# Extra matmuls on TensorE whose results nobody reads: behind every argument matmul, and in four places before, between and after other work

## The chip, the core and the metric

The kernel runs on one core of one Trainium2 chip. The metric is the device time of one execution in microseconds; lower is better. Engines are named as in the profile: PE is TensorE's matmuls, PEld its weight loads, DVE VectorE, ACT ScalarE, POOL GpSimd, SP SyncE. A line such as L748 is a line of the kernel before.

## The reference

Two branches over the same input `x` (2048 positions, 640 channels) are mixed by a gate per position. Branch A is attention with 32 heads of 20 channels, where each position sees 8 earlier ones at a distance of 2. Branch B is a state-space convolution: a kernel K of 2048 taps per channel is made from 192 complex modes, and is convolved with the input by FFT.

```python
g = sigmoid((x * gate_w).sum(-1, keepdims=True))
# A: q, k, v = x @ wqkv; 8 taps, dilation 2; softmax over the taps; @ wo
idx = pos[:, None] - off[None, :]            # off = arange(8) * 2
logits = einsum("bhsd,bhswd->bhsw", q, k[idx]) * scale
a = einsum("bhsw,bhswd->bhsd", softmax(logits), v[idx]) @ wo
# B: K[d, l] = Re sum_n C[d,n] exp(dt[d] A[d,n] l) dt[d] B[d,n]
P = exp((dt * A)[:, :, None] * arange(L))
K = einsum("dn,dnl,dn->dl", C, P, dt * B).real
b = irfft(rfft(pad(x)) * rfft(pad(K)))[:L] + x * Dskip
return g * a + (1 - g) * b
```

## The kernel before

**Two plans.** The program has two parts. The first holds the projections, the attention, the making of K and the first step of the transform. The second, `fft_conv`, holds the rest of the transform, the product of the spectra, the inverse and the mix. Each part is a list of tasks (`Plan.add`), each task with an engine (P is TensorE, A ScalarE, D VectorE, S and G the queues of SyncE and GpSimd), a function that issues its instructions, and tasks that it depends on. The order in which all tasks are issued is written out by hand as a list of task numbers, `SEQ1` for the first part and `SEQ2` for the second. Every engine runs its instructions strictly in that order. The numbers after a task's name (duration, `eq`, `due`) served to find an order, and change nothing in what is issued.

**The making of K.** The 80 channel groups are taken in 10 chunks (`NCH`). For each chunk, TensorE makes the arguments of sine and exponential functions by small matmuls (`args`, L747): the stationary operand is a slice of `L`, 64 rows and 128 columns, the moving operand a slice of the constant `R`. A task of kind 0 (sine) issues two matmuls of `SW` = 304 columns, one for each half of the array's rows, into the two banks of a tile `ar` of 2 x 512 fp32 values. A task of kind 1 (exponential) issues four of `EW` = 216 columns, two into each bank. There are 12 tasks of kind 0 and 6 of kind 1 in each chunk, 180 in all. ScalarE then evaluates the function from `ar` (`act`, L760 for the sine, L762 for the exponential) and writes into a ring of buffers. VectorE multiplies sine and exponential tiles (L783 to L785), and TensorE sums the products over the modes in many small matmuls on 32 columns of the array (L801).

There are two tiles `ar` at a time. They are also used for the transposes of the input (L200), for the gate's logits, and for the first step of the transform (`bp`, L1232). So TensorE can be at most two tiles ahead of the engine that reads them.

**The attention** runs in between. The projections are at L291 (tile `tb`, 512 columns, five accumulated matmuls for each tile). The logits (L357), the softmax's shift (L379) and its sum (L387) go to the tile `lg`, the sum over the taps (L426) and the output projection (L444) again to `tb`. `ident` is the identity matrix, 128 x 128.

**The shapes of the array.** A matmul of 128 rows and 128 columns is shown as 128*128. L748 uses 64 rows at a time (64*128, with `tile_position`), L801 and L357 use 32 columns, L426 uses 64 columns.

**The end of the first part.** K's two halves go through device memory (`Kx`, then `kc`), and the first step of the transform reads them from there (L1232). Then `fft_conv` starts with L1009.

## Time and profile before

| | |
|---|---|
| median of 3 runs | 362.78 us (361.1 to 363.49) |
| the profiled execution's own time | 360.97 us |
| its span, first to last instruction | 359.0 us |
| mean granted clock of TensorE | 0.961 |
| busy: PE, DVE, ACT, POOL | 293.7, 311.5, 303.0, 78.3 us |
| the 480 argument matmuls (L748) on PE | 55.3 us busy, idle before them 14.7 us |
| the sine activations (L760, 96 of 120) on ACT | 59.0 us busy, 681 ns each |
| the exponential activations (L762, 60) on ACT | 50.3 us busy, 917 ns each |

The busy time of an engine is the union of its instructions' times. A matmul's end is modelled, and matmuls overlap, so the distance between the starts of two groups tells more than the length of one. In the timelines, a row is a run of like instructions: its start, its length, the engine, the line, the operation, what it writes and reads with the shape of the array, the count, and in brackets how long the engine was idle before it and what ended that. In a row of groups, the numbers after the bar are the busy time in microseconds and the mean length of one instruction in nanoseconds, then the idle time before them. A row of waits tells who waited for whom: total time, how often, the longest.

### The profile page before, as it was taken

The page shows a single profiled execution, that of the slowest core. Times are in us where ns is not written, and L with a number is a line of the kernel's source. Part 1 is how long each engine was busy: PE and PEld are TensorE (multiplying, and loading weights), DVE is VectorE, ACT ScalarE, POOL GpSimd, SP SyncE. Part 2 cuts the span into 40 slices and gives each one's busy share as a digit, 9 for nine tenths or more (in the row PEclk, how much of TensorE's full clock was granted, in tenths as well). Part 3 has the DMA queues.
Part 4 walks back from the last instruction along what each step waited for, and adds up shares of the span by engine and source line. Part 5 has one row for each costly group of instructions (what it writes and reads, how often), then busy time and mean ns, then how long its engine had stood idle before and what let it go on. Part 6 is the DMA issues. An engine that isn't in the chain of part 4 may idle for free. (4 is left out here: it accounts for less than half of the span.)

```text
span 359.0 us, 12203 instructions
## 1 busy us (share of the span) xinstructions
PE 293.7 (82%) x5271; PEld 173.4 (48%) x5286; DVE 311.5 (87%) x413; ACT 303.0 (84%) x417; POOL 78.3 (22%) x125
## 2 busy tenths in 40 slices
PE   0199999699999999888887869999997799978760
PEld 0065564234544545445443424566664556647650
DVE  2899999669999899999998987999993479999982
ACT  1699997578989999999997979999895599888881
POOL 8930090211020100100012122416010023310032
PEclk9999999989999999999998978999998899999995
DMA  7951289421501611461256867489653149943047
GB/s 259 370 175 57 82 213 268 120 66 19 150 11 27 122 40 19 140 129 30 71 109 192 190 152 137 95 177 256 172 153 101 38 126 225 228 95 75 4 98 199
DMA packets 44042, 46.60 MB, mean 130 GB/s; under 512 B 24517, under 2 KB 38133, under 8 KB 43733
## 3 DMA queue, kind: packets, MB, share of 16 engines
q1 hardware_dynamic: 36116, 24.43, 26.2%
q0 software_dynamic: 5840, 20.55, 22.5%
q10 hardware_dynamic: 2032, 0.85, 0.9%
q8 instruction: 41, 0.67, 0.8%
q14 instruction: 13, 0.10, 0.1%
HBM read 31.31 MB, written 14.51 MB: 128 GB/s over the span
## 5 line engine op out<-in xcount | busy, mean ns | idle before, releaser
L291 PE MATMUL tb<-bufA 128*128 128x512 bf16 x285 | 71.7, 387 | 2.8 <-issue 1.1
L748 PE MATMUL ar<-Rarg,L 64*128 64x304 bf16 (+1 forms) x480 | 55.3, 282 | 14.7 <-ACT big L760 5.9
L760 ACT ACTIVATE big<-ar 128x608 bf16<-128x608 int16 x96 | 59.0, 681 | 8.2 <-PE ar L748 5.7
L762 ACT ACTIVATE big<-ar 128x864 bf16<-128x864 f32 x60 | 50.3, 917 | 3.6 <-PE ar L748 3.3
L291 PEld LDWEIGHTS <-bufA 128*128 128x128 bf16 x300 | 33.2, 120 | 31.7 <-issue 9.3
L420 DVE TENSOR_TENSOR pv<-vc,asb 128x4096 bf16<-128x4096 bf16 (+1 forms) x24 | 46.3, 1928 | 1.4 <-PE tb L426 1.4
L748 PEld LDWEIGHTS <-L 64*128 64x128 bf16 x480 | 21.4, 94 | 48.8 <-issue 41.9
L1009 PEld LDWEIGHTS <-PHI 128*128 128x128 bf16 x288 | 26.8, 99 | 18.0 <-issue 8.4
L801 PE MATMUL kps<-qq,pt 128*32 128x22 bf16 (+1 forms) x2560 | 26.3, 175 | 4.2 <-issue 4.2
L444 PE MATMUL tb<-wo_sb,oT 128*128 128x320 bf16 x160 | 28.1, 311 | 0.0
L801 PEld LDWEIGHTS <-pt 128*32 128x32 bf16 (+1 forms) x2560 | 22.5, 91 | 11.6 <-issue 8.7
L351 DVE TENSOR_TENSOR prod<-qk 128x2048 bf16<-128x2048 bf16 x20 | 24.1, 1220 | 2.9 <-PE lg L357 2.8
L351 DVE TENSOR_TENSOR prod<-prj 128x2048 bf16<-128x2048 bf16 x20 | 24.0, 1219 | 0.6 <-PE lg L357 0.5
L345 POOL DMA_DIRECT2D vc<-vS x16 | 11.5, 725 | 57.1 <-DVE pv L420 54.0
L426 PE MATMUL tb<-pv,ind 128*64 128x512 bf16 (+1 forms) x192 | 22.4, 361 | 0.2
L785 DVE TENSOR_TENSOR qq<-big 128x1408 bf16<-128x1408 bf16 x24 | 21.2, 885 | 0.0
L470 ACT ACTIVATE bufA<-bp 128x1024 bf16<-128x1024 f32 x16 | 16.0, 1032 | 5.6 <-PE bp L1232 5.5
L1009 PE MATMUL fp<-big,PHI 128*128 128x320 bf16 x112 | 17.9, 304 | 3.0 <-ACT sp_u L470 3.0
L200 PE MATMUL ar<-ident,xn 128*128 128x128 bf16 x80 | 8.1, 263 | 15.0 <-DMA xn<-in_A_x_dram 14.3
L470 ACT ACTIVATE sp_u<-fp 128x1280 bf16<-128x1280 f32 x14 | 17.3, 1237 | 3.4 <-PE fp L1009 3.4
L470 ACT ACTIVATE prj<-tb 128x512 bf16<-128x512 f32 x28 | 17.1, 612 | 3.1 <-PE tb L291 3.0
L470 ACT ACTIVATE big<-bp 128x1024 bf16<-128x1024 f32 x19 | 18.6, 1023 | 1.0 <-PE bp L1232 0.8
(173 smaller groups left out, 587.2 us busy)
## 6 DMA issues: line engine op xcount, KB each, us to landing
vc<-vS POOLq DMA_DIRECT2D x16, 327.5 KB, 6.9
PHI<-c_phi POOLq DMA_DIRECT2D x8, 384.0 KB, 4.9
Sprm<-pc SPq DMA_DIRECT2D x12, 240.0 KB, 2.0
L<-Sprm SPq DMA_DIRECT2D x80, 36.0 KB, 2.6
xn<-in_A_x_dram SPq DMA_DIRECT2D x4, 640.0 KB
gaS<-ga SPq DMA_DIRECT2D x8, 320.0 KB, 3.0
Usb<-in_A_x_dram POOLq DMA_DIRECT2D x8, 320.0 KB, 5.0
gaF<-gaS SPq DMA_DIRECT2D x8, 320.0 KB, 7.3
```

The costliest lines, as they stand in the source:

```text
L291: nc.tensor.matmul(ppf, self.wq[:, kt, which * D + e:(which + 1) * D:5], self.xT[:, c0 // 1024, kt, c0 % 1024:c0 % 1024 + SC], start=(kt = ...
L351: nc.vector.tensor_tensor(b[e][:], self.part(ch, 0)[:, e, o:o + C].unsqueeze(1).to_broadcast([128, W, C]), win(self.part(ch, 1)[:, e, :], ...
L420: nc.vector.tensor_tensor(b["pv", e][:, 0:2 * n], taps, aw, ALU.mult)
L426: nc.tensor.matmul(b["op", e][64 * a:64 * a + 64, 0:n, :], self.twin, b["pv", e][:, a:2 * n:2, w, :], start=(w == 0), stop=(w == HV - 1), ...
L444: nc.tensor.matmul(apf[:, :320], b["oT"][:, e, i * 128:(i + 1) * 128], wo_sb[:, e, hf * 320:(hf + 1) * 320], start=(e == 0), stop=(e == 4))
L470: nc.scalar.activation(o, i, ACT.Identity)
L748: nc.tensor.matmul(ar[:, g2, a0:a0 + ncol], L[rows, sb, gp, l0:l0 + 128], R[rows, c0:c0 + ncol], start=True, stop=True, tile_position=(64 ...
L760: nc.scalar.activation(dst[:, 2 * gp:2 * gp + 2, sub, :], ar[:].bitcast(I16)[:, :, 0:2 * SW:2], ACT.Sin, scale=SCL)
L762: nc.scalar.activation(dst[:, 2 * gp:2 * gp + 2].rearrange("p g s n -> p g (s n)"), ar[:, :, 0:2 * EW], ACT.Exp)
L785: nc.vector.tensor_tensor(qq[:], trg[:, :, KI:].rearrange("p a (v m) -> p a v m", v=2), exq[:, :, KI:].unsqueeze(2).to_broadcast([128, 32, ...
L801: nc.tensor.matmul(kps[32 * g:32 * g + 32, h, NM * ql:NM * ql + NM], pt[rows, k, v, :], qq[rows, k, v, :], start=(g not in started), stop= ...
L1009: nc.tensor.matmul(o.rearrange("p (c x) -> p c x", x=32), phis[fb][:, fl, kind, :], B[:, :, 2 * f1 + ri].rearrange("p c q g -> p c (q g)") ...
```

## The change

Behind the argument matmuls of each task comes, in the columns of the tile `ar` that stay free, a matmul with the identity as stationary operand and the constant `R` as moving operand: for kind 0 one of 512 - 304 = 208 columns in the second bank, for kind 1 one of 512 - 432 = 80 columns in each of the two banks. These use the whole array (no `tile_position`). Nobody reads what they write.

Besides, four new tasks (`fl0` to `fl3`, numbers 1090 to 1093 in `SEQ1`) each take a tile `ar` and write four matmuls of 512 columns into it. In the order, the first stands just ahead of the first argument task, the second and third behind the last group of L426, and the fourth at the end of the first part, behind the last L1232 and ahead of L1009. The rest of the order is the same; in the diff, the list is only broken into lines anew.

```diff
@@ SEQ1 @@
-... 517 244 563 562 245 518 520 268 ...
+... 517 244 563 562 245 1090 518 520 268 ...
-... 504 500A 1059A 1053A 505 503A 506D 1074 1070 ...
+... 504 500A 1059A 1053A 505 1091 1092 503A 506D 1074 1070 ...
-... 515 1078 1086 1079D 1087A
+... 515 1078 1086 1079D 1087A 1093
@@ args @@
                                         nc.tensor.matmul(ar[:, g2, a0:a0 + ncol], L[rows, sb, gp, l0:l0 + 128], R[rows, c0:c0 + ncol],
                                                          start=True, stop=True, tile_position=(64 * g2, 0))
+                                for g2 in (1,) if kind == 0 else (0, 1):
+                                    o = (SW, 2 * EW)[kind]
+                                    nc.tensor.matmul(ar[:, g2, o:512], self.ident[:], R[:, 0:512 - o], start=True, stop=True)
                                 b["ar", u, kind, gp, sub] = ar
@@ gated_mix_kernel @@
+        kg.ident = at.ident
         kg.plan(pl, pa, pk, lambda c: pr["g"][c], late[:30] + xdone[-1:], params, opened, fin)
...
+        def warm(_):
+            w = pa.tile([128, 2, 512], F32, name="ar")
+            for k in range(4):
+                nc.tensor.matmul(w[:, k % 2], at.ident[:], kg.R[:, 0:512], start=True, stop=True)
+        for n in range(4):
+            t = pl.add(f"fl{n}", "P", 0.85, warm, acq=["ar"], due=0.0, eq=2176)
+            t.rel = [("ar", t)]
         pl.emit(tc)
```

More of the change, by code (lines that the diff above doesn't have):

```diff
@@ L65 @@
 60 62D 122 146 85A 123A 57 147A 91A 125 129 230 126A 61 63 112 48 130A 113A 50 231 59 64A 152 154 153A 65A 155A 67 139 222 232 66 233 49 58 69 54 140A 68 70 55 71 72 234
-127 137 73 235 128A 236 143 237 138A 223 144A 516 238 133 265 239 131 134D 240 148 267 224 132A 241 242 150 225 149A 151A 226 243 266 269 517 244 563 562 245 518 520 268
-141 270 519 521 271 522 524 272 523 273 994 124 221 145 228 264 156 525 274 526 528 167 275 301 168D 142A 527 529 276 530 532 531 533 178 534 536 180 535 537 179A 303 538
@@ L68 @@
-540 539 541 175 181D 246 176D 186 542 544 277 278 543 545 187A 279 182 546 548 302 304 157 554 305 307 547 183A 549 158A 159 184 160A 306 308 550 552 551 553 185D 309 337
-173 280 609 281 608 227 177 188 310 564 566 171 311 174A 565 312 567 313 172A 161 314 568 570 162A 569 571 556 315 339 165 572 574 338 573 575 166D 341 555 340 576 577
-578 342 169 343 345 579 170A 163 580 582 199 581 583 584 586 585 587 557 344 346 558 588 590 589 591 200A 249 164D 559 347 600 373 203 592 594 593 204A 595 348 210 211A
@@ L71 @@
-205 560 596 598 206D 375 561 349 597 207 208D 350 201 351 189 602 599 202A 190A 610 612 611 613 601 374 376 377 614 616 247 615 617 379 618 620 191 248A 619 621 622 624
-378 380 197 623 192A 625 626 628 252 381 605 409 198A 627 629 603 604 630 631 632 606 633 634 635 382 636 216 212 411 383 607 637 213D 646 316 655 352 654 317 638 217A
-639 640 384 250 642 641 385 251A 643 644 645 214 386 656 648 387 195 215A 657 658 660 647 253 410 412 196A 659 661 254A 701 700 388 662 664 663 665 193 194A 282 651 413
@@ L74 @@
-666 667 668 255 257 670 256D 218 669 671 672 673 649 674 675 285 258D 415 219D 676 677 650 678 679 414 680 681 682 259 683 684 686 685 687 652 688 689 692 417 416 209 300
-690 418 702 691 703 704 261 705 260A 706 708 283 707 709 710 653 694 445 419 262A 288 711 712 693 714 713 715 284D 447 697 716 718 717 719 695 720 721 722 420 724 723 725
-755 756 263 353 726 727 286 289 728 729 730 696 732 731 733 734 698 421 735 318 287D 290D 738 699 736 291 737 757 758 759 760 739 761 762 422 763 765 764 766 740 423 743
@@ L77 @@
-292D 741 767 768 801 802 769 446 448 742 771 293 770 773 772 775 774 776 777 744 778 294A 779 781 295 780 782 783 784 449 321 745 793 451 795 746 785 787 786 789 297 788
-296A 790 791 803 792 804 805 450 806 807 794 809 808 811 298A 810 812 319 813 453 320A 814 815 796 816 817 818 452 819 820 821 454 823 822 824 825 826 798 749 324 455 481
-827 828 322 456 829 797 830 831 832 457 325 747 748A 833 458 834 835 799 836 837 323D 483 839 326A 750 459 800 424 847 848 299 389 751 894 893 460 220 336 372 752 849 327
@@ L80 @@
-838 850 851 482 852 841 485 853 484 854 855 840 857 856 858 859 486 861 860 487 328D 489 862 842 863 329 331 865 844 330D 864 866 867 869 488 868 871 870 873 843 872 874
-875 877 333 876 878 879 881 880 882 845 354 332D 885 846 887 883 884 895 897 490 896 899 898 901 886 900 903 902 905 355 334A 904 906 491 357 360 356D 890 907 908 909 910
-753 940 335 939 425 888 911 912 913 915 914 916 492 917 918 919 920 358 361 921 889 923 922 359D 362D 390 924 925 891 927 926 929 363 928 930 941 942 943 365 931 364D 892
@@ L83 @@
-366D 933 945 944 946 932 947 367 949 948 493 368D 950 951 952 369 953 391 955 393 934 392D 396 936 954 956 370A 935 494 957 371 754 995 996 997 408 998 999 1000 444 1001
-1002 958 959 394 960 961 963 397 395A 962 964 398A 937 965 967 966 968 399 1010 400A 1011A 401 969 1026 402A 970 403 971 405 495 938 977 979 404D 426 406D 429 1027A 972
-973 974 1024 1025A 978 1022 1023A 980 1014 1015A 1012 427 1013A 1028 1029A 461 496 407 428D 432 975 430 976 1018 431D 1019A 982 462 1016 433 434A 981 1020 435 1017A 1021A
@@ L86 @@
-1032 1033A 1030 437 1031A 1036 983 1037A 436D 1034 439 1064 438D 465 984 440D 985 1035A 1042 1065A 441 986 1043A 987A 1044 1066 1045A 1067A 463 1054 442D 988 989 464D 468
-1055A 497 443 990 1038 466 1004 1006 1009 1005 1008 1007 1003 480 991 993 1039A 1050 469 1062 467D 1051A 470D 1063A 498 1068 471 1040 473 1069A 1041A 472D 992 1046 1048
-475 474A 1047A 1049A 501 476A 477 1060 1056 1061A 478D 1057D 499 479 1058 1052 502 504 500A 1059A 1053A 505 503A 506D 1074 1070 507 1075A 1071D 1082 509 1080 508D 1083A
@@ L89 @@
-510D 1081A 511 1088 1084 512D 1089A 1085D 513 514A 1076 1072 1077D 1073A 515 1078 1086 1079D 1087A
+127 137 73 235 128A 236 143 237 138A 223 144A 516 238 133 265 239 131 134D 240 148 267 224 132A 241 242 150 225 149A 151A 226 243 266 269 517 244 563 562 245 1090 518 520
+268 141 270 519 521 271 522 524 272 523 273 994 124 221 145 228 264 156 525 274 526 528 167 275 301 168D 142A 527 529 276 530 532 531 533 178 534 536 180 535 537 179A 303
+538 540 539 541 175 181D 246 176D 186 542 544 277 278 543 545 187A 279 182 546 548 302 304 157 554 305 307 547 183A 549 158A 159 184 160A 306 308 550 552 551 553 185D 309
@@ new lines @@
+337 173 280 609 281 608 227 177 188 310 564 566 171 311 174A 565 312 567 313 172A 161 314 568 570 162A 569 571 556 315 339 165 572 574 338 573 575 166D 341 555 340 576
+577 578 342 169 343 345 579 170A 163 580 582 199 581 583 584 586 585 587 557 344 346 558 588 590 589 591 200A 249 164D 559 347 600 373 203 592 594 593 204A 595 348 210
+211A 205 560 596 598 206D 375 561 349 597 207 208D 350 201 351 189 602 599 202A 190A 610 612 611 613 601 374 376 377 614 616 247 615 617 379 618 620 191 248A 619 621 622
@@ new lines @@
+624 378 380 197 623 192A 625 626 628 252 381 605 409 198A 627 629 603 604 630 631 632 606 633 634 635 382 636 216 212 411 383 607 637 213D 646 316 655 352 654 317 638
+217A 639 640 384 250 642 641 385 251A 643 644 645 214 386 656 648 387 195 215A 657 658 660 647 253 410 412 196A 659 661 254A 701 700 388 662 664 663 665 193 194A 282 651
+413 666 667 668 255 257 670 256D 218 669 671 672 673 649 674 675 285 258D 415 219D 676 677 650 678 679 414 680 681 682 259 683 684 686 685 687 652 688 689 692 417 416 209
@@ new lines @@
+300 690 418 702 691 703 704 261 705 260A 706 708 283 707 709 710 653 694 445 419 262A 288 711 712 693 714 713 715 284D 447 697 716 718 717 719 695 720 721 722 420 724 723
+725 755 756 263 353 726 727 286 289 728 729 730 696 732 731 733 734 698 421 735 318 287D 290D 738 699 736 291 737 757 758 759 760 739 761 762 422 763 765 764 766 740 423
+743 292D 741 767 768 801 802 769 446 448 742 771 293 770 773 772 775 774 776 777 744 778 294A 779 781 295 780 782 783 784 449 321 745 793 451 795 746 785 787 786 789 297
@@ new lines @@
+788 296A 790 791 803 792 804 805 450 806 807 794 809 808 811 298A 810 812 319 813 453 320A 814 815 796 816 817 818 452 819 820 821 454 823 822 824 825 826 798 749 324 455
+481 827 828 322 456 829 797 830 831 832 457 325 747 748A 833 458 834 835 799 836 837 323D 483 839 326A 750 459 800 424 847 848 299 389 751 894 893 460 220 336 372 752 849
+327 838 850 851 482 852 841 485 853 484 854 855 840 857 856 858 859 486 861 860 487 328D 489 862 842 863 329 331 865 844 330D 864 866 867 869 488 868 871 870 873 843 872
@@ new lines @@
+874 875 877 333 876 878 879 881 880 882 845 354 332D 885 846 887 883 884 895 897 490 896 899 898 901 886 900 903 902 905 355 334A 904 906 491 357 360 356D 890 907 908 909
+910 753 940 335 939 425 888 911 912 913 915 914 916 492 917 918 919 920 358 361 921 889 923 922 359D 362D 390 924 925 891 927 926 929 363 928 930 941 942 943 365 931 364D
+892 366D 933 945 944 946 932 947 367 949 948 493 368D 950 951 952 369 953 391 955 393 934 392D 396 936 954 956 370A 935 494 957 371 754 995 996 997 408 998 999 1000 444
@@ new lines @@
+1001 1002 958 959 394 960 961 963 397 395A 962 964 398A 937 965 967 966 968 399 1010 400A 1011A 401 969 1026 402A 970 403 971 405 495 938 977 979 404D 426 406D 429 1027A
+972 973 974 1024 1025A 978 1022 1023A 980 1014 1015A 1012 427 1013A 1028 1029A 461 496 407 428D 432 975 430 976 1018 431D 1019A 982 462 1016 433 434A 981 1020 435 1017A
+1021A 1032 1033A 1030 437 1031A 1036 983 1037A 436D 1034 439 1064 438D 465 984 440D 985 1035A 1042 1065A 441 986 1043A 987A 1044 1066 1045A 1067A 463 1054 442D 988 989
@@ L90 @@
+464D 468 1055A 497 443 990 1038 466 1004 1006 1009 1005 1008 1007 1003 480 991 993 1039A 1050 469 1062 467D 1051A 470D 1063A 498 1068 471 1040 473 1069A 1041A 472D 992
+1046 1048 475 474A 1047A 1049A 501 476A 477 1060 1056 1061A 478D 1057D 499 479 1058 1052 502 504 500A 1059A 1053A 505 1091 1092 503A 506D 1074 1070 507 1075A 1071D 1082
+509 1080 508D 1083A 510D 1081A 511 1088 1084 512D 1089A 1085D 513 514A 1076 1072 1077D 1073A 515 1078 1086 1079D 1087A 1093
 """.split()
```

## The prediction

> **What bounds the kernel now.** I read the page first, then busy time by stage, then TensorE's own timeline inside the stages. From the page:

> ```profile
> span 359.0 us, 12203 instructions
> PE 293.7 (82%) x5271; PEld 173.4 (48%) x5286; DVE 311.5 (87%) x413; ACT 303.0 (84%) x417; POOL 78.3 (22%) x125
> ...
> PEclk9999999989999999999998978999998899999995
> ```

> Three engines stand between 82% and 87%, so none of them bounds the whole span, and the clock row shows only a few slices below 9. The windows cut the span where the character changes (columns: window, its length, busy time with the number of instructions of PE, PEld, DVE, ACT and POOL, clock, DMA share, GB/s):

> ```profile
> 60.00:75.00 15.00, 11.69 (x72) 4.45 (x71) 10.59 (x18) 7.83 (x13) 3.24 (x7) 0.89 0.50 137
> 75.00:121.00 46.00, 44.30 (x679) 22.12 (x683) 42.59 (x54) 41.26 (x63) 5.55 (x8) 1.00 0.23 55
> 121.00:190.00 69.00, 59.03 (x1604) 32.52 (x1596) 67.68 (x99) 67.45 (x104) 4.36 (x6) 1.00 0.38 86
> 190.00:227.00 37.00, 31.52 (x786) 15.84 (x787) 32.00 (x43) 32.20 (x46) 7.55 (x13) 0.86 0.70 163
> 227.00:250.00 23.00, 22.06 (x594) 14.21 (x593) 22.96 (x27) 22.52 (x33) 10.92 (x17) 1.00 0.75 178
> ...
> 268.00:284.00 16.00, 11.66 (x137) 7.75 (x136) 8.61 (x11) 9.59 (x11) 0.00 (x0) 0.86 0.30 96
> ```

> From 75 to 121 us TensorE is the bound: 44.30 of 46 us busy, idle 1.70. From 121 to 190 VectorE (67.68 of 69) and ScalarE (67.45) are full and TensorE has 9.97 us of idle time. From 190 to 227 TensorE has 5.48 us, from 227 to 250 only 0.94. All argument matmuls lie in these stages: the first row below is the first of them, the last row the last.

> ```profile
> 65.66 0.77 PE L748 MATMUL ar<-Rarg,L 64*128 64x304 bf16 x4 [1.69 <-DMA L<-Sprm]
> ...
> 243.95 0.31 PE L748 MATMUL ar<-Rarg,L 64*128 64x304 bf16 x2
> ```

> So the change adds work to the engine that bounds one stage, and that has 3.31 + 1.70 + 9.97 + 5.48 + 0.94 = 21.4 us of idle time in all the stages it touches.

> **What an argument task costs today.** Groups by form, then the timeline of PE at a place where nothing waits:

> ```profile
> L748 PE MATMUL ar<-Rarg,L 64*128 64x304 bf16 x240 | 34.9, 303 | 10.9 <-ACT big L760 5.7 <-DMA L<-Sprm 2.7 <-ACT bufA L760 0.7
> L748 PE MATMUL ar<-Rarg,L 64*128 64x216 bf16 x240 | 20.7, 262 | 3.8 <-ACT big L762 2.5 <-ACT big L760 0.3 <-ACT bufA L760 0.3
> ```

> ```profile
> 100.42 0.43 PE L748 MATMUL ar<-Rarg,L 64*128 64x304 bf16 x4
> 100.79 1.27 PE L291 MATMUL tb<-bufA 128*128 128x512 bf16 x5
> 101.99 0.43 PE L748 MATMUL ar<-Rarg,L 64*128 64x304 bf16 x4
> 102.36 0.65 PE L801 MATMUL kps<-qq,pt 64*32 64x22 bf16 x64
> ...
> 106.00 0.39 PE L379 MATMUL lg<-hi,ident 128*128 128x512 bf16 x1
> 106.22 0.38 PE L379 MATMUL lg<-lo,ident 128*128 128x512 bf16 x1
> 106.44 0.81 PE L291 MATMUL tb<-bufA 128*128 128x512 bf16 x3
> ```

> 240 + 240 matmuls are 120 sine tasks (kind 0, two matmuls) and 60 exponential tasks (kind 1, four). The last three rows have one shape of the array (128*128), and start 0.22 us apart for 512 columns: 0.43 ns per column, with nothing lost between different tiles or lines. The first rows change the shape. Two sine tasks (x4, where the two row halves run together) need 2 x 304 x 0.43 = 0.26 us, yet L291 starts 0.37 us after them: 0.11 us is lost on going from 64*128 to 128*128. Five L291 matmuls need 5 x 0.22 = 1.10 us, and the next argument task starts 1.20 us after them: 0.10 us on the way back. **This is the number on which the forecast turns**, as each added matmul is 128*128 and sits between 64*128 and whatever follows.

> [...]

> **The change part by part.** Nothing is removed.

> (a) *Extra columns.* A sine task gets one matmul of 512 - 304 = 208 columns: 208 x 0.43 = 0.089 us. An exponential task gets two of 512 - 432 = 80: 0.069 us. Weight loads of the identity I cost at nothing: in the L379 rows, whose weights are loaded for each matmul, the matmuls run without a gap; if that cover fails for 80 columns, it is a few hundredths of a us for each of 120.

> (b) *Added changes of shape.* They depend on what follows on TensorE. I counted the followers of the 180 tasks in PE's timeline between the two rows shown. If a 128*128 group follows (L291, L444, L379, L387), the change of shape was there already: no addition. If a column-tiled group follows (L801, L357, L426: 128*32, 64*32, 128*64), one is added; its price is not separable in the rows, I take 0.10 from the same neighbours (bounds 0 and 0.11). If another 64-row task follows, two are added: 0.21.

> By stage, tasks (sine + exponential) and followers (64-row / column-tiled / 128*128):
> 60 to 75: 8 + 0, 4/2/2: 0.7 + 0.84 + 0.2 = 1.7 us.
> 75 to 121: 26 + 12, 19/8/11: 3.1 + 4.0 + 0.8 = 7.9 us.
> 121 to 190: 50 + 29, 34/29/16: 6.5 + 7.1 + 2.9 = 16.5 us.
> 190 to 227: 24 + 19, 19/16/8: 3.4 + 4.0 + 1.6 = 9.0 us.
> 227 to 250: 12 + 0, 5/5/2: 1.1 + 1.05 + 0.5 = 2.6 us.
> Together 37.7 us of TensorE time against 21.4 us of idle time.

> (c) *What idle time takes up.* If every idle piece could be used, the overrun is 7.9 - 1.7 = 6.2, 16.5 - 10.0 = 6.5, 9.0 - 5.5 = 3.5 and 2.6 - 0.9 = 1.7 us, **17.9 us**; the first stage hides its own. Not all can be used. The idle pieces look like this, where ScalarE sets the pace:

> ```profile
> 198.53 4.90 ACT L760 ACTIVATE big<-ar 128x608 bf16<-128x608 int16 x8
> 199.26 0.31 PE L748 MATMUL ar<-Rarg,L 64*128 64x304 bf16 x2 [0.19 <-ACT big L760]
> ...
> 199.83 0.31 PE L748 MATMUL ar<-Rarg,L 64*128 64x304 bf16 x2 [0.26 <-ACT big L760]
> 200.40 0.31 PE L748 MATMUL ar<-Rarg,L 64*128 64x304 bf16 x2 [0.26 <-ACT big L760]
> ```

> There are two `ar` tiles. TensorE fills one for 0.31 us, waits 0.26 us until ScalarE frees the other, and the pair repeats every 0.57 us. The activation reads the banks which the extra matmul writes, so I take it to wait for the extra one too. An extra of 0.11 + 0.089 us fits in 0.26, but leaves about 0.06 us, and everything that is put in between (L801 for 0.65 us, L444) no longer fits. ScalarE's next activation is late by up to 0.2 us, then VectorE's product of those tiles, then the L801 group that reads it. Two of the waits can't be filled at all, as TensorE has nothing to issue in them:

> ```profile
> PE ar L748 <- ACT big L760: 5.9, 23, 0.3
> PE kps L801 <- issue: 3.8, 2, 2.1
> ```

> Of the 15.4 us of idle time in 121 to 227 I take a quarter as lost to fit, 4 us (bounds 0 and 15), so 22 us.

> (d) *The clock.* The windows of one us show where it is halved (the columns are those of the table of stages):

> ```profile
> 189.00:190.00 1.00, 0.00 (x0) 0.00 (x0) 0.68 (x1) 0.38 (x2) 0.43 (x1) 1.00 0.95 335
> ...
> 191.00:192.00 1.00, 1.00 (x5) 0.44 (x3) 1.00 (x2) 1.00 (x2) 0.00 (x0) 0.50 1.03 353
> ...
> 208.00:209.00 1.00, 0.00 (x0) 0.00 (x0) 0.93 (x4) 0.68 (x2) 0.00 (x0) 1.00 0.92 243
> ...
> 212.00:213.00 1.00, 1.00 (x68) 0.55 (x64) 1.00 (x1) 0.63 (x2) 0.69 (x1) 0.50 0.10 18
> ```

> Twice an empty us on TensorE is followed by half clock. The stage means make it 0.89 over 15 us and 0.86 over 37 us: lost clock 1.7 and 5.2 us. The empty places are the two "issue" waits above, which a matmul queued in the same stream can't fill, so I count a third of the 6.9 us: -2 us (bounds 0 and -6.9).

> (e) *The four warm tasks.* Four matmuls of 512 columns each, 4 x 0.22 = 0.88 us a task. The first stands ahead of the first argument task, in the wait for DMA of 1.69 us: hidden. The others:

> ```profile
> 268.92 1.49 PE L426 MATMUL tb<-pv,ind 128*64 128x512 bf16 x16
> 272.78 1.24 PE L1232 MATMUL bp<-F1c,kc 64*128 64x128 bf16 x16 [2.37 <-DMA kc<-Kx]
> 273.95 1.51 PE L444 MATMUL tb<-wo_sb,oT 128*128 128x320 bf16 x5
> ...
> 277.18 0.85 PE L444 MATMUL tb<-wo_sb,oT 128*128 128x320 bf16 x5
> ...
> 281.33 0.85 PE L1232 MATMUL bp<-F1c,kc 64*128 64x128 bf16 x16 [0.72 <-DVE bufA L472]
> 283.30 2.29 PE L1009 MATMUL fp<-bufA,PHI 128*128 128x320 bf16 x8 [1.11 <-ACT bufA L470]
> ```

> The second and third fill 1.76 of the 2.37 us ahead of 272.78, where TensorE waits for a transfer. Behind it L444 takes 1.51 us cold against 0.85 warm; if it stays warm, 0.66 + (1.24 - 0.85) = 1 us comes back. The fourth stands in the wait of 1.11 us ahead of L1009, but needs an `ar` tile that is freed only as that wait ends: up to 0.9 us later (1.8 at half clock). I set these against each other: 0.

> **The sum.** 17.9 + 4 - 2 + 0 = 20 us on the profiled execution's own 360.97 us: **381 us**. Its span is 359.0, with 2 us around it; the median of the three runs is 1.8 us above it, well inside the terms.

> **The rivals.**

> *Columns alone.* The drains fall together with waits, and only columns are paid: 3.1 - 1.7 = 1.4 us in 75 to 121, 0.2 in 227 to 250, nothing elsewhere; the activations that start within 0.19 us of their matmuls (87 of 180 in the timelines) each lose about 0.05 us, 4.4 us. 361 + 6 = 367 us. For it: in the loop at 199 the extra fits. Against it: from 75 to 121 there are no waits to fall into.

> *The clock repays it: faster.* One mechanism, in 71 to 75, 190 to 218 and 272 to 286 us: fuller windows keep the clock at 1.0. The loss to be regained is 6.9 us, plus 0.14 x 16 = 2.2 us in 268 to 284 and about 1 us in the first L1009 group (2.29 against some 1.25 once warm). It decides when over half of these 10 us lies on the path and the extras cost under 4 us net: 361 - 5 + 1 = 357 us. [...] Against the rival: the clock is 1.00 from 75 to 190 us, where 24.4 of the 37.7 us are added and nothing can be regained.

> *It does not matter.* VectorE and ScalarE are full from 121 to 190, extras hide under them, the clock stays as it is: 361 to 363 us.

> **Chances.** Forecast 0.62 (its own range 371 to 391: 17.9 with no loss to fit and half the drains at column-tiled followers, up to 15 us lost to fit), columns alone 0.20, faster 0.11, no matter 0.07. The range runs from 363, which leaves out the faster cases and part of the last, to 392. A measurement of this kernel tells about 1% (3.6 us) from no change: faster by more 0.11, within 0.08, slower by more 0.81.

> **What would show it.** Right: L748's followers start about 0.2 us later on TensorE, TensorE's idle time in the 75 to 121 stage is near zero and that stage is 6 us longer, 121 to 227 becomes TensorE-bound with VectorE and ScalarE waiting for `ar`, `lg` or `tb`. Wrong: argument groups one behind another at the old distance (activations not held, drains hidden), or a clock of 1.0 throughout with a shorter 190 to 227 stage.

## The result and the profile after

| | before | with the change |
|---|---|---|
| median of 4 runs | 362.37 us (361.1 to 363.49) | 383.98 us (380.54 to 387.85) |
| the profiled execution's own time | 360.97 us | 384.34 us |
| its span | 359.0 us | 382.3 us |
| mean granted clock of TensorE | 0.961 | 0.974 |

The kernel is slower by the ratio 1.0566, with an interval of 1.0483 to 1.0648: 21.6 us between the medians, 23.3 us between the spans. The forecast was 381 us. In the changed kernel the added argument matmul is L752; L760, L762, L801, L1009 and L1232 of before are now L763, L765, L804, L1012 and L1236.

From the page of the changed kernel, the span, the engines' busy time, the clock row, the queue q8, whose kind the page gives as instruction (packets, MB, share), and the added matmul's group:

```profile
span 382.3 us, 12730 instructions
...
PE 325.5 (85%) x5542; PEld 189.6 (50%) x5542; DVE 312.9 (82%) x413; ACT 308.5 (81%) x417; POOL 76.8 (20%) x125
...
PEclk9999999999999889999999999699999999999996
...
q8 instruction: 43, 0.70, 0.8%
...
L752 PE MATMUL ar<-Rarg,ident 128*128 128x208 bf16 (+1 forms) x240 | 46.6, 238 | 0.0
```

TensorE is busy for 32 us more. VectorE and ScalarE do the same work in the longer span. The clock is higher, not lower. This queue moved 43 packets; it was 41 before:

```profile
q8 instruction: 41, 0.67, 0.8%
```

The change adds 120 + 120 + 16 = 256 matmuls, each with a weight load: 512 instructions for TensorE, and q8 moved two packets more. That row turned out to matter more than it looks.

The waits of the changed kernel (engine, tile and line, what it waited for: total us, times, longest):

```profile
ACT big L765 <- PE ar L752: 12.6, 12, 2.8
ACT big L763 <- PE ar L752: 10.3, 20, 1.3
DVE prod L351 <- PE lg L357: 10.0, 7, 4.3
DVE ga L455 <- PE tb L444: 8.9, 8, 3.7
PE kps L804 <- issue: 5.0, 5, 2.4
```

The same two lines before:

```profile
ACT big L760 <- PE ar L748: 5.7, 7, 2.2
ACT big L762 <- PE ar L748: 3.3, 3, 1.4
```

Before, ScalarE waited 5.7 and 3.3 us for `ar` in these two lines. Now it waits 12.6 + 10.3 = 22.9 us, and VectorE waits for `lg` and `tb`: TensorE has become the engine that the others wait for, and an activation does wait for the extra matmul in its tile.

**Where the time went.** I took the activations of ScalarE in order (there are equally many in each kernel) and compared the end of one and the same activation in two traces. What it is later by, minus what it was later by at the start of a stage, is what the stage lost. Each kernel has one trace, so a row is one execution. Stages are named by the time in the kernel before; e1, e3, x2 and x3 are experiments told below.

| lost in the stage, us | to 75 | 75–121 | 121–190 | 190–227 | 227–250 | rest | span |
|---|---|---|---|---|---|---|---|
| predicted overrun | 0 | 6.2 | 6.5 | 3.5 | 1.7 | 0 | +20, with +4 and -2 not placed |
| the change | 0.1 | 4.7 | 14.1 | 3.5 | 2.6 | -1.7 | +23.3 |
| e1: extras, no warm tasks | 0.3 | 4.7 | 12.7 | 2.8 | 3.4 | -0.8 | +23.1 |
| e3: extras of the same shape | 0.1 | 1.0 | 10.5 | 3.5 | 1.0 | -3.5 | +12.6 |
| x2: before, with 128 instructions ahead | 0.2 | -0.9 | 8.7 | -5.5 | 3.6 | -1.2 | +4.9 |
| x3: the change, with 128 instructions ahead | 0.6 | 5.2 | 8.6 | -1.9 | 2.6 | 0.6 | +15.7 |

In 121 to 190 us the change lost twice what was forecast. TensorE's timeline of the changed kernel shows where most of that excess lies:

```profile
127.84 0.43 PE L804 MATMUL kps<-qq,pt 128*32 128x22 bf16 x37
130.68 0.37 PE L804 MATMUL kps<-qq,pt 128*32 128x22 bf16 x27 [2.42 <-issue]
...
132.84 4.47 PE L291 MATMUL tb<-bufA 128*128 128x512 bf16 x10
...
241.25 0.54 PE L748 MATMUL ar<-Rarg,L 64*128 64x216 bf16 x3 [2.64 <-issue]
```

A group of 64 equal matmuls stops after the 37th, and goes on 2.42 us later; nothing that the profile shows held it. After it, ten matmuls of 512 columns take 4.47 us, about 0.45 us each at a clock of 0.50, double the 0.22 us from start to start of L379's at 106.00 us before, at a clock of 1.00. The windows around the two places (columns as in the prediction):

```profile
75.00:127.50 52.50, 52.48 (x808) 25.93 (x805) 44.30 (x56) 42.05 (x63) 5.33 (x8) 1.00 0.27 62
126.00:137.50 11.50, 9.08 (x228) 4.03 (x219) 4.91 (x9) 5.76 (x8) 0.00 (x0) 0.70 0.16 31
137.50:208.00 70.50, 66.41 (x1534) 36.56 (x1530) 62.92 (x91) 64.48 (x96) 4.29 (x6) 1.00 0.30 70
239.00:247.00 8.00, 5.75 (x73) 2.49 (x74) 2.54 (x5) 3.04 (x5) 1.38 (x4) 0.57 0.19 45
```

The first row is the stage that the prediction called 75 to 121: TensorE's idle time there is gone (52.48 of 52.50). In the second row the clock is 0.70 over 11.5 us, so 3.4 us of clock are lost besides the 2.42 us of standing still; together 5.8 us, and between 121 and 131 us of the old time the activations fall back by 6.3. Between them, from 137.5 to 208 us, TensorE is busy for 66.41 of 70.5 us, more than VectorE (62.92) and ScalarE (64.48), which were full here before. The last row has a place like the first again: 2.64 us standing, and 0.43 x 8 = 3.4 us of clock. Before, there were two such places too, at 190 and 210 us:

```profile
187.88 0.63 PE L801 MATMUL kps<-qq,pt 128*32 128x22 bf16 x61
190.22 0.19 PE L801 MATMUL kps<-qq,pt 128*32 128x22 bf16 x3 [1.72 <-issue]
...
209.82 0.45 PE L801 MATMUL kps<-qq,pt 128*32 128x22 bf16 x39 [2.08 <-issue]
```

In the changed kernel these are gone, and the two at 130 and 241 are new.

### The profile page after: what moved, and what is told of

It is laid out like the page before. It is cut to its first block, busy times and chain, and to the rows that moved or that the text cites. A ratio compares the mean times of both kernels' runs of the same rounds, so it can differ in the third digit from the quotient of the medians.

```text
span 382.3 us, 12730 instructions
## 1 busy us (share of the span) xinstructions
PE 325.5 (85%) x5542; PEld 189.6 (50%) x5542; DVE 312.9 (82%) x413; ACT 308.5 (81%) x417; POOL 76.8 (20%) x125
## 3 DMA queue, kind: packets, MB, share of 16 engines
q1 hardware_dynamic: 36116, 24.43, 24.3%
## 5 line engine op out<-in xcount | busy, mean ns | idle before, releaser
L291 PE MATMUL tb<-bufA 128*128 128x512 bf16 x300 | 73.8, 388 | 1.9 <-ACT pv L470 0.9
L763 ACT ACTIVATE big<-ar 128x608 bf16<-128x608 int16 x96 | 60.9, 676 | 11.9 <-PE ar L752 10.3
L748 PE MATMUL ar<-Rarg,L 64*128 64x304 bf16 (+1 forms) x480 | 59.9, 283 | 10.8 <-ACT big L763 3.3
L765 ACT ACTIVATE big<-ar 128x864 bf16<-128x864 f32 x60 | 50.6, 897 | 13.5 <-PE ar L752 12.6
L291 PEld LDWEIGHTS <-bufA 128*128 128x128 bf16 x300 | 33.8, 119 | 29.7 <-issue 7.0
L752 PE MATMUL ar<-Rarg,ident 128*128 128x208 bf16 (+1 forms) x240 | 46.6, 238 | 0.0
L748 PEld LDWEIGHTS <-L 64*128 64x128 bf16 x480 | 21.5, 94 | 41.7 <-issue 30.7
L1012 PEld LDWEIGHTS <-PHI 128*128 128x128 bf16 x288 | 26.2, 97 | 16.7 <-issue 8.3
L752 PEld LDWEIGHTS <-ident 128*128 128x128 bf16 x240 | 18.3, 97 | 28.4 <-issue 12.0
L804 PE MATMUL kps<-qq,pt 128*32 128x22 bf16 (+1 forms) x2560 | 26.6, 175 | 5.0 <-issue 5.0
L444 PE MATMUL tb<-wo_sb,oT 128*128 128x320 bf16 x160 | 28.0, 311 | 0.0
L804 PEld LDWEIGHTS <-pt 128*32 128x32 bf16 (+1 forms) x2560 | 22.6, 91 | 10.0 <-issue 7.0
L345 POOL DMA_DIRECT2D vc<-vS x16 | 11.5, 724 | 69.2 <-DVE pv L420 66.7
L426 PE MATMUL tb<-pv,ind 128*64 128x512 bf16 (+1 forms) x192 | 21.3, 349 | 0.0
L470 ACT ACTIVATE sp_k<-fp 128x1280 bf16<-128x1280 f32 x14 | 17.3, 1237 | 4.9 <-PE fp L1012 4.6
L470 ACT ACTIVATE prj<-tb 128x512 bf16<-128x512 f32 x28 | 16.9, 604 | 5.3 <-PE tb L291 4.9
L470 ACT ACTIVATE bufA<-bp 128x1024 bf16<-128x1024 f32 x16 | 16.1, 1025 | 4.7 <-PE bp L1236 4.6
```

Source lines behind the costliest of these rows:

```text
L291: nc.tensor.matmul(ppf, self.wq[:, kt, which * D + e:(which + 1) * D:5], self.xT[:, c0 // 1024, kt, c0 % 1024:c0 % 1024 + SC], start=(kt = ...
L426: nc.tensor.matmul(b["op", e][64 * a:64 * a + 64, 0:n, :], self.twin, b["pv", e][:, a:2 * n:2, w, :], start=(w == 0), stop=(w == HV - 1), ...
L444: nc.tensor.matmul(apf[:, :320], b["oT"][:, e, i * 128:(i + 1) * 128], wo_sb[:, e, hf * 320:(hf + 1) * 320], start=(e == 0), stop=(e == 4))
L470: nc.scalar.activation(o, i, ACT.Identity)
L748: nc.tensor.matmul(ar[:, g2, a0:a0 + ncol], L[rows, sb, gp, l0:l0 + 128], R[rows, c0:c0 + ncol], start=True, stop=True, tile_position=(64 ...
L752: nc.tensor.matmul(ar[:, g2, o:512], self.ident[:], R[:, 0:512 - o], start=True, stop=True)
```

## The experiments

Theories: **shape** (the array's shape changes around each extra matmul cost TensorE time, as forecast), **columns** (only its columns cost), **clock** (extras and warm tasks change the clock's record, for better or worse), and later **instructions** (the added instructions shift the stream that TensorE reads, and so where it has to wait for it). What the prediction and the expectation of e1 call a drain is the 0.10 to 0.11 us lost at a change of shape in the rows from 100.42 to 101.99 us before; what TensorE does in that time no run shows.

**e1: the extras without the four warm tasks.** The loop over the warm tasks and their four numbers in the order are taken out.

```diff
-        for n in range(4):
+        for n in range(0):
```

> The 240 extra matmuls behind the argument tasks, without the four warm tasks. Shape theory (each extra adds changes of the array's shape that drain TensorE): nearly all of the loss is here, +20 to +23 us against before. Clock theory (the warm tasks bring something at the end): about 1.5 us slower than the whole change, since the first step of the transform and the first L1009 group fall back to half clock. Issue theory (it is the number of instructions on TensorE that costs): +20 us.

385.08 us, ratio 1.0654 (1.0612 to 1.0695). The loss is all in the extras.

**e2: the four warm tasks without the extras.**

```diff
-                                for g2 in (1,) if kind == 0 else (0, 1):
-                                    o = (SW, 2 * EW)[kind]
-                                    nc.tensor.matmul(ar[:, g2, o:512], self.ident[:], R[:, 0:512 - o], start=True, stop=True)
```

> The four warm tasks alone, no extra matmul behind an argument task. Shape theory and clock theory alike: 0 to -2 us against before (1.2 us from the second and third, 0.4 from the fourth, nothing from the first). If the wait for an ar tile of the fourth weighs more: +0.5 to +1 us.

362.69 us, ratio 1.0022 (0.9973 to 1.0072): no difference. The warm tasks, by themselves, are neither the loss nor a gain.

**e3: the extras in the shape of their neighbours.** The same number of matmuls with the same columns into the same place, but with 64 rows and the weights of the argument; no warm tasks.

```diff
-                                    nc.tensor.matmul(ar[:, g2, o:512], self.ident[:], R[:, 0:512 - o], start=True, stop=True)
+                                    rows = slice(64 * g2, 64 * g2 + 64)
+                                    nc.tensor.matmul(ar[:, g2, o:512], L[rows, sb, gp, l0:l0 + 128], R[rows, 0:512 - o],
+                                                     start=True, stop=True, tile_position=(64 * g2, 0))
```

> The same extra columns behind each argument task, but as 64-row matmuls like the argument matmuls themselves (weights from L, same place in the array), no warm tasks: as many instructions, as many columns, the activations still wait for them, no change of shape. Shape theory: +2 to +6 us, since 240 matmuls cost 0.089 us for a sine task and 0.035 to 0.069 for an exponential one, 13 to 15 us in all, most of it in idle time. Column theory (streaming and the held activation cost, not the shape): +12 to +20 us. Issue theory: +20 us, as in the kernel with args alone.

374.5 us, ratio 1.0354 (1.0326 to 1.0382). Against e1, on the same chip, shape is worth 10.6 us. TensorE's timeline of the changed kernel and then of e3, at two sine tasks and the L291 group behind them (in e3 the extra is L753):

```profile
101.90 0.30 PE L748 MATMUL ar<-Rarg,L 64*128 64x304 bf16 x2
102.14 0.26 PE L752 MATMUL ar<-Rarg,ident 128*128 128x208 bf16 x1
102.33 0.30 PE L748 MATMUL ar<-Rarg,L 64*128 64x304 bf16 x2
102.57 0.26 PE L752 MATMUL ar<-Rarg,ident 128*128 128x208 bf16 x1
102.67 1.24 PE L291 MATMUL tb<-bufA 128*128 128x512 bf16 x5
103.84 0.30 PE L748 MATMUL ar<-Rarg,L 64*128 64x304 bf16 x2
```

```profile
100.36 0.43 PE L748 MATMUL ar<-Rarg,L 64*128 64x304 bf16 x3
100.50 0.25 PE L753 MATMUL ar<-Rarg,L 64*128 64x208 bf16 x1
100.59 0.29 PE L748 MATMUL ar<-Rarg,L 64*128 64x304 bf16 x1
100.72 0.25 PE L753 MATMUL ar<-Rarg,L 64*128 64x208 bf16 x1
100.90 1.27 PE L291 MATMUL tb<-bufA 128*128 128x512 bf16 x5
102.11 0.43 PE L748 MATMUL ar<-Rarg,L 64*128 64x304 bf16 x3
```

From the first task to the next argument task behind L291 it was 1.57 us before (100.42 to 101.99). It is 1.94 with the change, 0.37 more; the prediction's prices give 2 x 0.089 + 0.21 = 0.39. In e3 it is 1.75, 0.18 more: just the columns. In 75 to 121, where no wait for instructions disturbs, e3 loses 1.0 us and e1 4.7. But over the whole, e3 loses 12.6 us, and 7.4 of them between 121 and 131:

```profile
123.54 0.46 PE L805 MATMUL kps<-qq,pt 128*32 128x22 bf16 x41
...
128.92 0.34 PE L805 MATMUL kps<-qq,pt 128*32 128x22 bf16 x23 [4.92 <-issue]
```

A wait of the kind seen above, of 4.92 us (L805 is L801 of before). Neither shape nor columns explains it.

**e4: whole-array extras of 16 columns.** The change of shape stays, the columns go; no warm tasks.

```diff
-                                    nc.tensor.matmul(ar[:, g2, o:512], self.ident[:], R[:, 0:512 - o], start=True, stop=True)
+                                    nc.tensor.matmul(ar[:, g2, o:o + 16], self.ident[:], R[:, 0:16], start=True, stop=True)
```

> Whole-array extra matmuls at the same 180 places, but of 16 columns instead of 208 and 80; no warm tasks. Shape theory: most of the loss stays, +11 to +17 us. Column theory: +2 to +6 us. Issue theory: +20 us.

380.64 us, ratio 1.0546 (1.0466 to 1.0625). Most of the loss stays without the columns. It is more than the +11 to +17 us expected of shape alone; this kernel too has waits of the kind above, the longest of 3.12 us ending at 130.80 us. TensorE's timeline of e4 has the shape's price nearly bare:

```profile
102.81 0.30 PE L748 MATMUL ar<-Rarg,L 64*128 64x304 bf16 x2
103.05 0.18 PE L752 MATMUL ar<-Rarg,ident 128*128 128x16 bf16 x1
...
103.44 1.25 PE L291 MATMUL tb<-bufA 128*128 128x512 bf16 x5
```

Two tasks now take 0.63 us up to L291, where they took 0.37: 0.26 us for two changes of shape and 32 columns.

**e5, e6, e7: the extras only behind some tasks**, by what follows on TensorE: only ahead of 128*128 groups (39 tasks, 56 extra matmuls), only ahead of another 64-row task (81, 103), only ahead of a column-tiled group (60, 81). `NOW` holds the name of the next task of TensorE in the order, and `kind_of` tells its shape; e6 and e7 have "rows" and "columns" in place of "full".

```diff
-                                for g2 in (1,) if kind == 0 else (0, 1):
+                                for g2 in () if kind_of(NOW[0]) != "full" else (1,) if kind == 0 else (0, 1):
```

> Extra matmuls only behind those 39 argument tasks that are followed by a 128*128 group on TensorE (56 matmuls), no warm tasks. Shape theory: no change of shape is added, only 22 x 0.089 + 17 x 0.069 = 3.1 us of columns, 0 to +2 us. Column theory: a fifth of the loss, +4 us.

> Extra matmuls only behind those 81 tasks that are followed by another 64-row task (103 matmuls), no warm tasks. Shape theory: two changes each, 81 x 0.21 + 6.6 us of columns = 23.6 us of TensorE time, the largest part, +9 to +14 us. Column theory: in proportion to the matmuls, 103/240 of the loss, +8 to +9 us.

> Extra matmuls only behind those 60 tasks that are followed by a column-tiled group (81 matmuls), no warm tasks. Shape theory: one change each at the price that the prediction could not separate (0 to 0.11 us), 6.0 + 4.9 us of TensorE time, +3 to +6 us. Column theory: 81/240 of the loss, +7 us.

366.86 us, ratio 1.0193 (1.0086 to 1.0301); 376.25 us, 1.045 (1.0347 to 1.0553); 366.19 us, 1.0159 (1.0087 to 1.023). The order is the forecast's, with the 64-row followers by far the dearest, and the three together (5.2 + 14.6 + 4.5 = 24.3 us over their before's median of 361.69) come near e1's 23.4. The sum is loose: by the ratios the three make 8.0%, and e1 6.5%. Yet e5, which adds no change of shape, came out slower than the 0 to +2 us expected (its interval begins at 0.9%), though its profiled span is only 1.3 us longer than before's. The three differ in more than shape: each shifts the instruction stream in its own way. In the trace of each, TensorE's waits for instructions lie at other places: counted over all of TensorE's instructions in the trace in order (matmuls, weight loads and a few for semaphores), those of over 1.1 us lie at numbers 2498, 6082 and 7873 in e5, 2498, 6850 and 7362 in e6, 6850 and 7873 in e7. In the changed kernel they lie at 2498 and 7107, in e3 at 2498, 6338 and 7106. Their distances are multiples of 256, to within one. Before, they lie at 5299 and 6067, three times 256 apart; that trace lacks 15 matmuls (5271 beside 5286 weight loads), and with these the numbers are 5314 and 6082, at a multiple of 256 from the others. And 10,557 instructions in 41 packets (before) are 257 a packet. So a new theory, worked out from these counts: TensorE's instructions come in **blocks of 256**, one packet of q8 each, and a wait comes where a block is late.

**x4: same shape and only 16 columns.** If shape and columns were all, nothing would be left to lose.

```diff
+                                    nc.tensor.matmul(ar[:, g2, o:o + 16], L[rows, sb, gp, l0:l0 + 128], R[rows, 0:16],
+                                                     start=True, stop=True, tile_position=(64 * g2, 0))
```

> Same-shape extras of 16 columns: as many instructions as the kernel with same-shape extras and at the same places in the stream, next to no columns, no change of shape, no warm tasks. Block theory: the waits at about 129 and 235 are there again, +6 to +11 us. Column theory: 0 to +3 us.

374.15 us, ratio 1.0402 (1.0334 to 1.0469): as slow as e3, with almost nothing to compute, and above both expectations. Nothing is lost up to 121 us (0.0), and then 6.1 us by 131, in TensorE's timeline at the same place in the same group as in e3:

```profile
122.41 0.46 PE L805 MATMUL kps<-qq,pt 128*32 128x22 bf16 x41
...
126.90 0.34 PE L805 MATMUL kps<-qq,pt 128*32 128x22 bf16 x23 [4.03 <-issue]
```

**x2: the kernel before, with 128 instructions at its start.** 64 matmuls of 16 columns, each with its weight load, in the first wait for the input. Nothing else is changed; half a block is put ahead of everything.

```diff
+    pad = pa.tile([128, 2, 512], F32, name="ar")
+    for k in range(64):
+        nc.tensor.matmul(pad[:, k % 2, 0:16], at.ident[:], at.ident[:, 0:16], start=True, stop=True)
```

> The kernel before, with the same 128 instructions in the wait at the start and nothing else. Block theory: its two waits for instructions (1.72 us ending at 190.22, 2.08 us ending at 209.82) move or go; the time goes anywhere from -6 (both gone, with the half clock behind them) to +6 us (one like the 4.92 us comes in). Other theories: no change, within 1 us.

367.85 us, ratio 1.0153 (1.0084 to 1.0223). The kernel is slower, though all that it added lies in a wait (0.2 us later at 75 us). TensorE's timeline of x2:

```profile
121.64 0.43 PE L801 MATMUL kps<-qq,pt 128*32 128x22 bf16 x37
...
126.69 0.37 PE L801 MATMUL kps<-qq,pt 128*32 128x22 bf16 x27 [4.62 <-issue]
```

The wait is in the group where the changed kernel has it, split the same way, 37 and 27; before has none there. And the two waits of before at 190 and 210 us are gone, which gives 5.5 us back in 190 to 227. The count explains the split. Ahead of this place the changed kernel has put 60 extra matmuls and the first warm task's four, with their weight loads 128 instructions, as many as the pad of x2. In e3 and x4 it is the 60 extras alone, 120 instructions, and the group is split four matmuls, eight instructions, later (41 and 23). Likewise e2, whose first warm task adds eight instructions, has the wait at 190 us four matmuls earlier in its group than before (57 and 7, for 61 and 3). So in these traces the place of a wait follows the count of instructions ahead of it, whatever put them there.

**x1: e3 with the same 128 instructions at its start.** The pad is that of x2.

> The kernel with same-shape extras, and 64 small matmuls more (128 instructions, 16 columns each) in TensorE's wait for the first transfers, about 2 us of the 12 us that it waits there. They only move the instruction stream by half a block of 256. In the unpadded kernel two waits of TensorE for instructions (4.92 us ending at 128.92, 2.61 us ending at 235.00, both at instruction numbers that are 194 modulo 256) sit where its delay jumps by 7.4 and 4.6 us. Block theory (the jumps are these waits and the half clock behind them, and move with the block's edge): the waits at 129 and 235 go, others may come; +3 to +9 us against before instead of +12.8. Column theory: unchanged, +12 to +13 us with the jumps in place.

367.58 us, ratio 1.0206 (1.0132 to 1.028), where e3 has 1.0354. The waits of e3 at 129 and 235 us are not in its trace, where the longest for instructions is 1.4 us.

**x3: the whole change with the same 128 instructions.**

> The whole change, with the same 128 instructions at the start. Block theory: its waits at 130.68 and 241.25 move or go; shape changes stay: +14 to +24 us against before, and the curve of the delay without the jumps of 6.3 and 5.5 us at these places. Shape theory alone: as the change, +21 to +23 us, jumps in place.

377.56 us, ratio 1.048 (1.0402 to 1.0558): instructions were added, and it took less time than the changed kernel in its own runs (1.0566), though the intervals overlap and the two were not measured beside the same runs of before. The profiled spans differ by 7.6 us. Of the page of x3, and of its waits, the longest ones that nothing shown ended:

```profile
span 374.7 us, 12858 instructions
...
PEclk9999999999999999999999999999999899999995
```

```profile
PE bp L1239 <- issue: 1.1, 1, 1.1
PE kps L804 <- issue: 1.0, 2, 0.7
```

No wait for instructions over 1.1 us is left in the stages of the change, and the clock row has no gap from 121 to 250 us. Ahead of the group that waits at 130 us in the changed kernel, x3 has 128 + 128 = 256 instructions more than before, a whole block: as before, no edge falls into the group, and there is no wait. What remains, 15.7 us, is the change without long waits, against a kernel before that still has its own two.

**x5: the kernel before with 256 instructions at its start**, a whole block, so that every edge falls where it fell before, one block later.

```diff
+    for k in range(128):
```

> The kernel before with 128 small matmuls in the wait at the start, 256 instructions, that is one whole block of 256 instead of half a block. Block theory: the block edges lie at the same places of the program as in the kernel before, so its own two waits (about 1.7 and 2.1 us, ending near 190 and 210 us) are there again, the wait of 4.62 us near 127 is gone, and the time is within 1% of before. If the padding itself costs (more instructions, longer start): +5 us or more, as with half a block or beyond.

365.5 us, ratio 1.0109 (1.0031 to 1.0186), against x2's 1.0153. TensorE's timeline:

```profile
192.07 0.21 PE L801 MATMUL kps<-qq,pt 128*32 128x22 bf16 x4 [2.14 <-issue]
...
250.64 1.06 PE L1235 MATMUL bp<-F1c,Usb 64*128 64x128 bf16 x15 [2.66 <-issue]
```

The wait at 127 is gone and the one at 190 is back, at the end of the same group (60 matmuls and 4; before, 61 and 3); the one at 210 isn't. It is missing in e2 as well, whose edges lie only eight instructions from those of before, so an edge alone doesn't make a wait. The longer pad costs 2.7 us up to 75 us, yet at 245 us this kernel stands 0.7 us ahead of before. Then comes a wait of 2.66 us that is not at an edge, with a slower TensorE behind it (five L444 matmuls take 1.52 us at 251.63, and 0.85 at 246.91), and the span ends 4.6 us longer. What it waits for isn't settled; a transfer into `Usb`, which L1235 reads there, was issued at 245.89 us, but the trace doesn't tie the two together. So the theory of blocks has the waits at 127 and 190 right and the one at 210 wrong, and the total doesn't return to that of before.

The two causes in one table (ratios to before; each row moves the stream, each column adds to the work):

| | before | same-shape extras | whole-array extras |
|---|---|---|---|
| stream as it comes | 1 | 1.0354 (e3), 1.0402 (x4) | 1.0654 (e1), 1.0566 (the change) |
| 128 instructions ahead | 1.0153 (x2) | 1.0206 (x1) | 1.048 (x3) |

From the second column to the third it is 3.0% in the first row (e1) and 2.7% in the second: about 10 us of shape, at both positions of the stream. From the first to the second it is 3.5 to 4.0% in one row and 0.5% in the other, with intervals that overlap there: most of what same-shape extras seem to cost in the first row is the stream's position, not the work.

## Why the prediction was right, and where its mechanism was not the whole

The time and its sign came out: 381 us forecast, 384 measured. Step by step:

- **(a) Columns.** Right in size: e3's two tasks took 0.18 us more for 2 x 208 columns (2 x 0.089). Their weight loads cost nothing that shows there.
- **(b) Changes of shape.** Right: 0.37 us against 0.39 for the pair ahead of L291. The price that the rows could not separate, at a column-tiled follower, is in the changed kernel's timeline:

```profile
104.51 0.26 PE L752 MATMUL ar<-Rarg,ident 128*128 128x208 bf16 x1
104.70 0.65 PE L804 MATMUL kps<-qq,pt 64*32 64x22 bf16 x64
```

  0.19 us, of which 0.09 are columns: 0.10, the value taken.
- **(c) The overrun.** 75 to 121 lost 4.7 us (6.2 forecast). In 121 to 190 x3, free of long waits for instructions, lost 8.6: 6.5 and a part of the 4 lost to fit. In 190 to 227 x3 gained 1.9 us; if the 5.5 that x2 gained there without extras is the worth of before's two waits, the extras cost 3.6 (3.5 forecast). So TensorE's part of the sum held.
- **What failed** is the sentence in (c) on the two waits "issue": that they "can't be filled at all", and so stay. No run shows whether they could be filled, but with 512 more instructions they moved: the two of 1.72 and 2.08 us at 190 and 210 went, and two of 2.42 and 2.64 us came, at 130 and 241. The change lost 14.1 us in 121 to 190 instead of some 9, and against x3 the span is 7.6 us longer. This term was missing from the sum. It shows little in the total, as the first stage cost 1.5 us less than forecast, the rest of the span gave back 1.7, and what the old waits had cost came back in 190 to 227. That 381 came so close to 384 is in part luck: a term that was missing met others that were too large.
- **(d) The clock.** -2 was for fuller windows. Those of the old waits did fill (the clock row has no gap at 190 to 220), but only because the waits went; half clock came back at the new ones (0.50 from 131 to 137 and from 241 to 246 us). The mean clock rose from 0.961 to 0.974 in a kernel that got 5.7% slower.
- **(e) The warm tasks.** 0 was right (e2, 1.0022). By its parts: the first L1009 group ran at a clock of 1.00, in 1.25 us as the row below shows, for 2.29 at 0.50 before, but the `bp` group ahead of it began 2.95 us before it and not 1.97, for the fourth task stands in between; the second and third were hidden.

```profile
304.84 0.86 PE L1236 MATMUL bp<-F1c,kc 64*128 64x128 bf16 x16 [0.72 <-DVE bufA L472]
...
307.79 1.25 PE L1012 MATMUL fp<-bufA,PHI 128*128 128x320 bf16 x8
```

- **The rivals.** *Columns alone* had 1.4 us for 75 to 121, and e3, in which only columns are added, lost 1.0 there; but the changes of shape are paid on top. *The clock repays it* fell: the mean clock rose, and the kernel got slower by 5.7%. That fuller windows keep the clock at 1.0 was the author's estimate from the half clock behind the empty microseconds in (d). *It does not matter* fell with ScalarE's 22.9 us of waiting for `ar`.
- **What would show it.** L748's followers came 0.2 us later, TensorE had no idle time left in the first stage, and ScalarE and VectorE wait for `ar`, `lg` and `tb` behind it, as said.

What stays open: whether 512 more instructions cost something by their number, besides their position; the wait at 250 us in x5; why some packets of q8 come late, and whether a wait comes in every execution of a kernel, as each has one trace; and what other positions of the edges would give. Only two positions of the change and three of the kernel before were measured. No kernel here beat the one before: the best, e2, is within 0.3% of it, with an interval on both sides of 1. An extra into a tile that no activation waits for was not tried.

## What to carry to other kernels

Price added TensorE work by the changes of the array's shape that it brings, read from the start-to-start distances of neighbours in the trace; here a change cost as much as 240 columns. Before a gain or loss of a few per cent is put down to an edit that adds or removes instructions, shift the unchanged kernel by some harmless instructions at its start and look for waits that nothing ends: here such a shift alone cost 1.5%. The extra instructions covered no such wait here: they moved the old ones, and two longer ones came, with half clock behind them.

## What the runs showed of the hardware that was not expected

The four packets with a long wait behind them came where the DMA engines were busy with other queues: in the microsecond behind the entry their share was 1.05 and 0.80 before, and 1.12 and 1.08 in the changed kernel. The windows of the changed kernel before and after its late packet at 128.1 us (the last but one number is the DMA share, a sum of the packets' times, which can exceed 1):

```profile
126.00:127.00 1.00, 1.00 (x130) 0.98 (x121) 1.00 (x3) 0.85 (x2) 0.00 (x0) 1.00 1.14 228
...
129.00:130.00 1.00, 0.00 (x0) 0.00 (x0) 0.00 (x0) 1.00 (x1) 0.00 (x0) 1.00 0.00 0
```

Between 70 and 260 us in the traces of before and of the changed kernel, 28 packets started 0 to 1.25 us after the entry, and in the microsecond behind the entry the DMA share of the other queues was 0.10 (median); 8 started 2.5 us or more after it, with a share of 0.95. That these transfers hold the instructions up is not shown: no run here took them away.

Most packets have no such wait behind them: before, two of 41 have one of over 1.1 us, in the changed kernel two of 43. The longest in the traces took 4.9 us (e3), and the ten microseconds around one lost 6.3 us in the changed kernel and 7.4 in e3, half clock included.

That the shape of the array costs 0.10 us at a change to column tiling as well, and that extra columns of the same shape in a tile that ScalarE reads cost little, were the two smaller surprises: e3 and x4 differ by 192 and 64 columns a matmul, and take 374.5 and 374.15 us; only from 75 to 121 us do the columns show, with 1.0 us.
